# Splitting numbers into a high and a low part: bit masks on VectorE against rounded copies on ScalarE

## The chip, the cores and the metric

The kernel runs on one core of a Trainium2 chip. The metric is the device time of one execution in microseconds (us), the median of several runs. Engines are called as in the profile: PE (TensorE, matmuls), PEld (its weight loads), DVE (VectorE), ACT (ScalarE), POOL (GpSimd), SP (the engine whose queue issues most DMAs).

## The reference

Two blocks follow each other. The first is block-wise linear attention with decay over q, k, v of shape (4 batches, 8 heads, 768 positions, 64 channels). The second is a mixer: a low-rank product along the sequence, added to its input, and a two-layer perceptron over the 512 channels.

```python
for b in range(nb):                                  # attention, blocks of 64
    intra = einsum('bhic,bhjc->bhij', qb, kb) * Dmask
    intra = einsum('bhij,bhjd->bhid', intra, vb)
    inter = einsum('bhid,bhde->bhie', qb * lam_pow, kv_state)
    out[:, :, sl] = intra + inter
    kv_state = lam_block * kv_state + einsum('bhsd,bhse->bhde', kb * rev_pow, vb)
x = out.transpose(0, 2, 1, 3).reshape(4, 768, 512)
u = x + ((x.transpose(0, 2, 1) @ U) @ V).transpose(0, 2, 1)      # rank 32
return u + maximum(u @ w_ch1, 0) @ w_ch2                         # 512 -> 2048 -> 512
```

U, V, w_ch1 and w_ch2 come as 64-bit floats and are brought to 32 bits in the kernel by integer operations on their words.

## The kernel before

**Split products.** The two large products run in the type float32r, which keeps fewer bits of the mantissa than float32. To keep the precision, each operand is split into a high part, which float32r holds exactly, and a low part. Three matmuls replace one: high by high and low by low terms, scaled by E = 2^-12, are gathered in one PSUM bank (`pz`), and a third product of combined parts, `diff` (scaled again by 4096 at the end), in another (`pd`). The high part is made by a bit mask: `tensor_scalar(..., HI, bitwise_and)` with HI = 0xFFFFF000 on VectorE. Splits are made of the weights (`split_steps`: `five` masks, `six` subtracts, `seven` combines), of the transposed input u of the first product (`turn`), and of the hidden values between the two products (`split(i)` near the end).

**Stages.**

1. Attention, from the start to about 113 us. The 24 tiles of 128 positions (4 batches of 6) are 24 steps s; c is the tile's number within its batch. A list written out by hand, `pieces`, fixes the order of instructions on every engine. A step of TensorE runs: transposes of the next tile's q and k (`pqk`, line 363), transposes of an earlier, finished tile (`turn`, line 613) and its neighbour's mix with the low-rank rows (`mix`, line 564), both into one pair of PSUM banks (`pm`), then `intra` (`px`, 452), `state` (`pkv`, 430), `inter` (`px`, 463), `scores` of the next tile (`pss`, 411). From s = 8 to 23 each step has a turn.
2. VectorE in such a step: `masked` (two halves of `sm`, line 420), the mask of the split (633), its subtraction `low` (634), `mixed` (576: x_nat plus the upper halves of `pm`), the new state `kv` (438, or 436 at c = 0), and then, in some steps, an operation of `aside`, a piece of weight preparation. ScalarE: copies of `qt` and `kt` (369), `fade` (404, four small scalings that `kv` needs), weight activations put off to `late`, `x_nat` (469), the scaled high part (620). POOL: `qs` (395), `ks` (384), and `diff` (621), issued by the piece `turned`. At c = 0 there are casts of the low-rank rows (`spread`, 532) as well.
3. `turn` for groups below FG = 4 writes the split of four tiles each into `u_hl` (high and low) and `u_d` (`diff`), laid out as channel block by 512 positions. The last batch's turns (line 595 on) lie between matmuls of the first product and have a bank `put` of their own.
4. First product, to about 420 us: `hidden(ft, pair)` for 16 blocks of hidden channels and three pairs of groups; sums `r` go to DRAM. Weights are prepared beside it.
5. Second product, to the end: `r` comes back, `split(i)` makes `m` (relu, high, low, combined), and `product` adds up 16 blocks.

The PSUM tiles `pkv` and `pqk` share a tag from the second batch on, so the transposes of a step wait until `kv` has read its bank. `tmp` is a ring of three buffers for pieces of splits and for the low-rank rows `p_f` and `p_h`. The weight pieces of the attention stage have their steps in lists:

```python
        (w1_steps(0, True), (3, 4, 5, 6, 8, 9, 10, 11, 13, 14, 15)),
        (w1_steps(1, True, True), (8, 9, 10, 11, 16, 17, 19, 20, 21, 22, 23, NS)),
```

The first four entries of each are loads; then follow `one` (165 and 154; apart in the second list), `two` (183), `three` (191), `four` (196), `five` (214), `six` (222), `seven` (229). ScalarE's part of `one` (172, 173) and of `five` (217) runs one step later, in `late`.

Of the kernel before, what the change touches and what calls it, by code (L numbers as in the profile page):

```python
# [18 lines left out]
def kernel(  # L19
# [43 lines left out]
    TG = N // P  # L63
    HI = 0xFFFFF000
    E = 2.0**-12


    EDGE = 352
# [17 lines left out]
    def on_scalar(what):  # L86
        if late and late[0] is None:
            late.append(what)
        else:
            what()  # L90
# [10 lines left out]
    w2_d = [dram.tile([P, 3, C], FP32, name=f"w2_d{ft}") for ft in range(FT)]  # L101

    def tmp(name):
        return wconv.tile([P, C], FP32, tag="tmp", bufs=3, name=name)

# [94 lines left out]
    def split_steps(tile_of, src, in_parts=False, scale=None, apart=False):  # L202

        st = {}

        def dst():
            if "w" not in st:
                st["w"] = wconv.tile([P, C], FP32, tag="wf", name="wf")
            return st["w"]

        def five():
            st["t"] = t = wconv.tile([P, C], FP32, tag="wt", name="wt")
            st["o"] = o = tile_of()
            nc.vector.tensor_scalar(  # L214
                t.bitcast(U32), st["w"].bitcast(U32), HI, None, ALU.bitwise_and
            )
            on_scalar(lambda: nc.scalar.copy(o[:, 0, :], t))  # L217

        def six():
            w, low = st["w"], st["o"][:, 1, :]  # L220
            st["low"] = low.bitcast(FP32) if scale is None else w
            nc.vector.tensor_tensor(
                out=low if scale is None else w, in0=w, in1=st["t"], op=ALU.subtract
            )
            if scale is not None:
                on_scalar(lambda: nc.scalar.mul(low, w, scale))

        def seven():
            nc.vector.scalar_tensor_tensor(
                st["o"][:, 2, :], st["t"], -E, st["low"], ALU.mult, ALU.add  # L230
            )

        return weight_steps(dst, src, C, in_parts=in_parts, apart=apart) + [five, six, seven]
# [342 lines left out]
        nc.vector.tensor_tensor(out=x, in0=pm, in1=x, op=ALU.add)  # L576

    uhl, ud, turned = {}, {}, {}
    hl_at, d_at = [hl_pool], [d_pool]

    def store(s):
# [2 lines left out]
    def turn(s):  # L584

        g, n = divmod(s, TG)
        if n == 0:
            uhl[g] = hl_at[g >= FG].tile([P, 2, CT, N], F32R, tag="hl", name="u_hl")
            ud[g] = d_at[g >= FG].tile([P, CT, N], F32R, tag="d", name="u_d")
        cols = slice(n * P, (n + 1) * P)  # L590
        hi, low, diff = uhl[g][:, 0, :, cols], uhl[g][:, 1, :, cols], ud[g][:, :, cols]
        if g >= FG:
            pt = bank([P, CT, P], "put", "b1")
            for ct in range(CT):
                nc.tensor.transpose(  # L595
                    out=pt[:, ct, :], in_=xs[s][:, ct * P : (ct + 1) * P], identity=ident
                )
            store(s)
            del xs[s]
            t = tmp("ut").rearrange("p (c n) -> p c n", n=P)  # L600
            nc.vector.tensor_scalar(t.bitcast(U32), pt.bitcast(U32), HI, None, ALU.bitwise_and)

            nc.vector.scalar_tensor_tensor(diff, t, 1.0 + E, pt, ALU.mult, ALU.subtract)
            uf = tmp("uf").rearrange("p (c n) -> p c n", n=P)
            nc.scalar.mul(hi, t, E)
            nc.scalar.copy(uf, pt)
            nc.gpsimd.tensor_tensor(out=low, in0=uf, in1=t, op=ALU.subtract)
            return

        pt = both_halves(s + 1)[:, :, 0 : 2 * P].rearrange("p t (c i) -> p t c i", i=D)  # L610
        for ct in range(CT):
            for n in range(2):
                nc.tensor.transpose(  # L613
                    out=pt[:, n, ct, :], in_=xs[s][half[n], ct * P : (ct + 1) * P],
                    identity=ident[half[n], half[n]],
                )
        del xs[s]

        def rest():
            nc.scalar.mul(hi, t, E)  # L620
            nc.gpsimd.tensor_tensor(
                out=diff, in0=hi.bitcast(FP32), in1=low.bitcast(FP32), op=ALU.subtract
            )

        def parts_of(what):
            return what.rearrange("p c (t i) -> p t c i", t=2)

        t = tmp("ut").rearrange("p (c n) -> p c n", n=P)
        split_t = parts_of(t.bitcast(U32))
        turned[s] = rest  # L630

        def split():
            nc.vector.tensor_scalar(split_t, pt.bitcast(U32), HI, None, ALU.bitwise_and)
            nc.vector.tensor_tensor(
                out=parts_of(low), in0=pt, in1=parts_of(t), op=ALU.subtract
            )

        splits[s] = split
# [4 lines left out]
    for s in range(NS):  # L643
        b, c = divmod(s, NT)
        done = s - NT - 1
        more = s + 1 < NS
        turns = done > 0 and (done - 1) // TG < FG
        mixes = 0 <= done < NS - NT - 1
        rows = c == 0 and b > 0
        step = [("prep", s + 1)] * more  # L650
        step += [("turn", done - 1)] * turns + [("mix", done)] * mixes
        step += [("mix", done + 1)] * (not more)
        step += [("next_of_low", b - 1)] * rows + [("next_of_low", b - 1)] * rows
        step += [("scale", s + 1)] * more
        step += [("fade", s)] * (c > 0)
        step += [("late", s - 1)] * (1 < s < NT - 1 or s > NT)
        step += [("turned", done - 2)] * (done > 1 and c == 1)
        step += [("split", done - 1)] * turns
        step += [("mixed", done)] * mixes + [("mixed", done + 1)] * (not more)
        step += [("next_of_low", b - 1)] * rows  # L660
        both = [("intra", s), ("state", s)]
        step += (both if s > NT else both[::-1]) + [("next_v", s), ("inter", s)]
        step += [("late", s)] * (s < 2 or s in (NT - 1, NT))
        step += [("turned", done - 1)] * (done > 0 and c > 0)
        step += [("scores", s + 1)] * more
        step += [("low", b)] * (more and c == NT - 1)
        step += [("aside", s)] * (0 < s < NT - 2 or s > NT)
        step += [("masked", s + 1)] * more
        step += [("low_rows", b)] * (more and c == NT - 1)
        step += [("aside", s)] * (s in (0, NT - 2, NT - 1, NT))  # L670
        step += [("store", done)] * (done >= 0 and done // TG < FG)
        pieces += step
# [136 lines left out]
    def hidden(ft, pair, before={}):  # L809

        acc = dict(zip(pair, banks(len(pair), next(turns))))
        count = iter(range(12 * len(pair)))

        def others():
            for what, s in before.get(next(count), ()):
                run[what](s)

        w = w1v[ft].rearrange("p n (c f) -> p n c f", f=P)
        for ct in range(CT):
            for n in range(2):  # L820
                for g in pair:
                    others()
                    nc.tensor.matmul(  # L823
                        out=acc[g][0], lhsT=w[:, n, ct, :], rhs=uhl[g][:, n, ct, :],
                        start=(ct == 0 and n == 0), stop=(ct == CT - 1 and n == 1),
                    )
        rs = {g: r_pool.tile([P, N], FP32, tag="r", name="r") for g in pair}
        for g in pair:
            nc.scalar.mul(rs[g], acc[g][0], 4096.0 + 1.0)  # L829
        for ct in range(CT):  # L830
            for g in pair:
                others()
                nc.tensor.matmul(  # L833
                    out=acc[g][1], lhsT=w[:, 2, ct, :], rhs=ud[g][:, ct, :],
                    start=(ct == 0), stop=(ct == CT - 1),
                )
        for g in pair:
            nc.vector.scalar_tensor_tensor(rs[g], acc[g][1], 4096.0, rs[g], ALU.mult, ALU.add)  # L838
            nc.sync.dma_start(out=r_d[ft][g], in_=rs[g])
# [92 lines left out]

    def split(i):
        r = rs.pop(i)
        t = m_pool.tile([P, N], FP32, tag="t", bufs=2, name="mt")
        ms[i] = m = m_pool.tile([P, 3, N], F32R, tag="m", name="m")
        hi, low = m[:, 0].bitcast(FP32), m[:, 1].bitcast(FP32)
        nc.vector.tensor_scalar(t.bitcast(U32), r.bitcast(U32), HI, None, ALU.bitwise_and)  # L938
        nc.scalar.activation(out=m[:, 0], in_=t, func=AF.Relu)  # L939
        nc.vector.scalar_tensor_tensor(m[:, 1], r, 0.0, hi, ALU.max, ALU.subtract)  # L940
        nc.vector.scalar_tensor_tensor(m[:, 2], hi, E, low, ALU.mult, ALU.subtract)  # L941

# [117 lines left out]
```

## Time and profile before

| | |
|---|---|
| Time, median of 3 runs | 650.72 us (649.88 to 652.89) |
| Span of the profiled execution | 648.7 us (its own time is not listed apart) |
| PE busy | 639.9 us, 99% |
| VectorE busy | 489.3 us, 75% |
| ScalarE busy | 279.8 us, 43% |
| POOL busy | 115.5 us, 18% |
| Granted TensorE clock | 1.000 |

The page of the profile gives busy times, a picture in 40 slices, the chain of waits that ended last and the costliest groups of instructions. Behind it stand views of the same trace: windows (busy times by stretch), waits (who waited for whom), and the timeline, whose lines read: start in us, duration in us, engine, line of the kernel, operation, output<-inputs, count, and in brackets the idle time before it and what ended it. A line may gather several instructions in a row on one engine. An instruction's duration may overlap the start of the next.

### The profile page before, as it was taken

To read this page: it belongs to the slowest core of one execution; us is meant where nothing else is said; L and a number is where in the kernel's file an instruction comes from. 1 tells how busy PE (TensorE), PEld (TensorE's weight loads), DVE (VectorE), ACT (ScalarE), POOL (GpSimd) and SP (SyncE) were. 2 spreads that over 40 slices of the span, in tenths; PEclk is the share of its full clock that TensorE was granted. 3 is DMA by queue.
4 is the path that set the end of the run, shared out by engine and by line. 5 is a ranking of instruction groups with operands and counts; after the bars stand their busy time and mean duration, and the time that the engine had idled before them with its cause. 6 is when DMAs were issued, how large, how long until landed. Compare 5 with 4: busy or idle time off the path is not lost.

```text
span 648.7 us, 13400 instructions
## 1 busy us (share of the span) xinstructions
PE 639.9 (99%) x5242; PEld 538.0 (83%) x5242; DVE 489.3 (75%) x862; ACT 279.8 (43%) x530; POOL 115.5 (18%) x98
## 2 busy tenths in 40 slices
PE   9999999999999999999999999999999999999997
PEld 8888989888888888888888888888888888888886
DVE  5579989878999777777797265796677776876864
ACT  4677877554656444444464221332322322322320
POOL 4466868340000000000000000030030300300300
PEclk9999999999999999999999999999999999999999
DMA  9999984354776656566687999855373353453531
GB/s 229 243 239 260 241 206 120 112 194 156 265 266 243 220 209 208 207 211 212 210 292 275 337 321 389 294 181 150 113 213 112 118 199 106 162 162 98 162 99 65
DMA packets 131776, 131.29 MB, mean 202 GB/s; under 512 B 81346, under 2 KB 89794, under 8 KB 131714
## 3 DMA queue, kind: packets, MB, share of 16 engines
q1 hardware_dynamic: 106592, 124.02, 59.7%
q10 hardware_dynamic: 25122, 6.42, 4.4%
q8 instruction: 41, 0.67, 0.4%
q14 instruction: 21, 0.17, 0.1%
HBM read 80.09 MB, written 50.33 MB: 201 GB/s over the span
## 4 chain that ended last, share of the span: by engine, by line
PE 96%; DVE 1%; ACT 1%; DMA 1%; issue 1%; ACTq 0%; DVEq 0%
PE pz L823 27%; PE pd L833 13%; PE pz L956 13%; PE pz L958 13%; PE pd L960 13%; PE pss L411 4%; PE px L452 4%; PE pqk L363 2%; PE px L463 2%; PE pkv L430 1%; PE pp L479 1%; PE pm L564 1%; DMA kraw<-in_k_dram 1%; PE put L595 1%; PE pm L613 0%
## 5 line engine op out<-in xcount | busy, mean ns | idle before, releaser
L823 PE MATMUL pz<-u_hl,w 128*128 128x512 f32 x768 | 184.7, 390 | 0.0
L823 PEld LDWEIGHTS pz<-u_hl,w 128*128 128x128 f32 x768 | 143.5, 188 | 30.4 <-ACT r L829 0.3
L958 PE MATMUL pz<-w_hl,m 128*128 128x512 f32 x384 | 148.3, 389 | 0.0
L956 PE MATMUL pz<-w_hl,m 128*128 128x512 f32 x384 | 148.1, 389 | 0.0
L960 PE MATMUL pd<-w_d,m 128*128 128x512 f32 x384 | 146.7, 389 | 0.0
L939 ACT ACTIVATE m<-mt 128x512 fp32r<-128x512 f32 x96 | 60.6, 632 | 188.3 <-PE pd L960 93.0
L985 POOL TENSOR_TENSOR o<-o,u 128x512 f32<-128x512 f32 x20 | 29.7, 1518 | 432.4 <-DVE o L981 432.4
L838 DVE SCALAR_TENSOR_TENSOR r<-pd,r 128x512 f32<-128x512 f32 x96 | 61.6, 683 | 47.9 <-ACT r L829 41.2
L833 PE MATMUL pd<-u_d,w 128*128 128x512 f32 x384 | 95.9, 390 | 0.0
L940 DVE SCALAR_TENSOR_TENSOR m<-rm,m 128x512 fp32r<-128x512 f32 x96 | 71.2, 744 | 32.4 <-ACT m L939 32.3
L829 ACT ACTIVATE r<-pz 128x512 f32<-128x512 f32 x96 | 52.2, 595 | 87.6 <-PE pz L823 87.6
L960 PEld LDWEIGHTS pd<-w_d,m 128*128 128x128 f32 x384 | 72.1, 188 | 15.3 <-DVE o L981 0.2
L956 PEld LDWEIGHTS pz<-w_hl,m 128*128 128x128 f32 x384 | 72.1, 188 | 15.0
L958 PEld LDWEIGHTS pz<-w_hl,m 128*128 128x128 f32 x384 | 72.1, 188 | 14.8
L833 PEld LDWEIGHTS pd<-u_d,w 128*128 128x128 f32 x384 | 71.8, 188 | 14.8
L938 DVE TENSOR_SCALAR mt<-rm 128x512 uint32<-128x512 uint32 x96 | 46.2, 482 | 39.2 <-DMA rm<-r_d 38.2
L941 DVE SCALAR_TENSOR_TENSOR m<-m 128x512 fp32r<-128x512 f32 x96 | 69.3, 724 | 0.9
L420 DVE TENSOR_TENSOR sm<-pss,mask 128x512 f32<-128x512 f32 x48 | 30.8, 684 | 9.6 <-PE pss L411 9.4
L217 ACT CAST w<-wt 128x512 fp32r<-128x512 f32 x32 | 19.9, 621 | 29.1 <-DVE wt L214 22.4
L452 PE MATMUL px<-vraw,sm 128*64 128x64 f32 x768 | 28.5, 228 | 2.6 <-ACT x_nat L469 1.2
L452 PEld LDWEIGHTS px<-vraw,sm 128*64 128x64 f32 x768 | 25.6, 140 | 5.6 <-ACT x_nat L469 1.5
L411 PE MATMUL pss<-qt,kt 64*128 64x128 f32 x384 | 28.8, 291 | 0.0
(96 smaller groups left out, 668.1 us busy)
## 6 DMA issues: line engine op xcount, KB each, us to landing
r_d<-r SPq DMA_DIRECT2D x96, 256.0 KB, 2.5
rm<-r_d SPq DMA_DIRECT2D x96, 256.0 KB, 2.7
words<-in_moe_w_ch_dram SPq DMA_DIRECT2D x30, 512.0 KB, 4.3
w_d<-w SPq DMA_DIRECT2D x16, 768.0 KB, 3.4
w_hl<-w_d SPq DMA_DIRECT2D x16, 512.0 KB, 6.3
u_d<-x_nat SPq DMA_DIRECT2D x24, 256.0 KB, 4.0
u<-u_d SPq DMA_DIRECT2D x24, 256.0 KB, 4.3
qraw<-in_q_dram SPq DMA_DIRECT2D x23, 256.0 KB, 4.2
```

The lines of the kernel that those rows point to most:

```text
L411: nc.tensor.matmul(out=pss[:, x, a, :], lhsT=kt[half[x], a, :], rhs=qt[half[x], a, :], start=True, stop=True,)
L452: nc.tensor.matmul(out=px[half[t], x, a, :], lhsT=sm[:, x, a, half[t]], rhs=vr[:, 2 * a + x, :], start=(a == 0), stop=(alone and a == HP - 1),
L823: nc.tensor.matmul(out=acc[g][0], lhsT=w[:, n, ct, :], rhs=uhl[g][:, n, ct, :], start=(ct == 0 and n == 0), stop=(ct == CT - 1 and n == 1),)
L829: nc.scalar.mul(rs[g], acc[g][0], 4096.0 + 1.0)
L833: nc.tensor.matmul(out=acc[g][1], lhsT=w[:, 2, ct, :], rhs=ud[g][:, ct, :], start=(ct == 0), stop=(ct == CT - 1),)
L838: nc.vector.scalar_tensor_tensor(rs[g], acc[g][1], 4096.0, rs[g], ALU.mult, ALU.add)
L939: nc.scalar.activation(out=m[:, 0], in_=t, func=AF.Relu)
L940: nc.vector.scalar_tensor_tensor(m[:, 1], r, 0.0, hi, ALU.max, ALU.subtract)
L941: nc.vector.scalar_tensor_tensor(m[:, 2], hi, E, low, ALU.mult, ALU.subtract)
L956: nc.tensor.matmul(out=pz, lhsT=m[:, 0, cols], rhs=hl[:, 0], start=first, stop=False)
L958: nc.tensor.matmul(out=pz, lhsT=m[:, 1, cols], rhs=hl[:, 1], start=False, stop=end)
L960: nc.tensor.matmul(out=pd, lhsT=m[:, 2, cols], rhs=dd, start=first, stop=end)
```

## The change

The mask goes. ScalarE multiplies the value by NEAR = 1 - 2^-13 and writes it into the float32r tile, which rounds it; VectorE subtracts that from the value for the low part.

- Weights: `five` loses its mask and its buffer `wt`; ScalarE's copy becomes a multiply that reads the weight itself; `six` and `seven` read the high part from the output tile.
- Hidden values: ScalarE's relu reads `r` directly, with scale NEAR; the mask and its buffer go.
- Turns of the attention stage: ScalarE writes the high part straight from PSUM, VectorE makes `low` from it and the same PSUM tile. Both now stand in the piece `split`; before, ScalarE's multiplication stood in `turned`, behind `x_nat`. In `pieces`, `mixed` and `split` move ahead of `fade` and `late`, with `mixed` first.
- Turns of the last batch: high on ScalarE from PSUM, `low` on VectorE (before: POOL, from a ScalarE copy), `diff` on POOL (before: VectorE).
- Layout: for groups 0 to 3 the split tiles hold eight runs of 64 positions, each run with its four channel blocks. The moving operand of the first product's matmuls is then eight runs of 64 columns instead of 512 in a row.
- The ring `tmp` has two buffers instead of three.

```diff
     def tmp(name):
-        return wconv.tile([P, C], FP32, tag="tmp", bufs=3, name=name)
+        return wconv.tile([P, C], FP32, tag="tmp", bufs=2, name=name)
...
         def five():
-            st["t"] = t = wconv.tile([P, C], FP32, tag="wt", name="wt")
             st["o"] = o = tile_of()
-            nc.vector.tensor_scalar(
-                t.bitcast(U32), st["w"].bitcast(U32), HI, None, ALU.bitwise_and
-            )
-            on_scalar(lambda: nc.scalar.copy(o[:, 0, :], t))
+            st["t"] = o[:, 0, :].bitcast(FP32)
+            on_scalar(lambda: nc.scalar.mul(o[:, 0, :], st["w"], NEAR))
...
+    def by_halves(what):
+        return what.rearrange("p c n -> p (c n)").rearrange("p (t c i) -> p t c i", c=CT, i=D)
+
+    def columns(what, g, ct):
+        return what[:, ct, :] if g >= FG else by_halves(what)[:, :, ct, :]
...
-            t = tmp("ut").rearrange("p (c n) -> p c n", n=P)
-            nc.vector.tensor_scalar(t.bitcast(U32), pt.bitcast(U32), HI, None, ALU.bitwise_and)
-
-            nc.vector.scalar_tensor_tensor(diff, t, 1.0 + E, pt, ALU.mult, ALU.subtract)
-            uf = tmp("uf").rearrange("p (c n) -> p c n", n=P)
-            nc.scalar.mul(hi, t, E)
-            nc.scalar.copy(uf, pt)
-            nc.gpsimd.tensor_tensor(out=low, in0=uf, in1=t, op=ALU.subtract)
+            nc.scalar.mul(hi, pt, E * NEAR)
+            nc.vector.scalar_tensor_tensor(
+                low, hi.bitcast(FP32), -1.0 / E, pt, ALU.mult, ALU.add
+            )
+            nc.gpsimd.tensor_tensor(
+                out=diff, in0=hi.bitcast(FP32), in1=low.bitcast(FP32), op=ALU.subtract
+            )
             return
...
         def rest():
-            nc.scalar.mul(hi, t, E)
             nc.gpsimd.tensor_tensor(
                 out=diff, in0=hi.bitcast(FP32), in1=low.bitcast(FP32), op=ALU.subtract
             )
...
         def split():
-            nc.vector.tensor_scalar(split_t, pt.bitcast(U32), HI, None, ALU.bitwise_and)
-            nc.vector.tensor_tensor(
-                out=parts_of(low), in0=pt, in1=parts_of(t), op=ALU.subtract
+            nc.scalar.mul(hi, both, E * NEAR)
+            nc.vector.scalar_tensor_tensor(
+                low, hi.bitcast(FP32), -1.0 / E, both, ALU.mult, ALU.add
             )
...
         step += [("scale", s + 1)] * more
+        step += [("mixed", done)] * mixes
+        step += [("split", done - 1)] * turns
         step += [("fade", s)] * (c > 0)
         step += [("late", s - 1)] * (1 < s < NT - 1 or s > NT)
         step += [("turned", done - 2)] * (done > 1 and c == 1)
-        step += [("split", done - 1)] * turns
-        step += [("mixed", done)] * mixes + [("mixed", done + 1)] * (not more)
+        step += [("mixed", done + 1)] * (not more)
...
-                        out=acc[g][0], lhsT=w[:, n, ct, :], rhs=uhl[g][:, n, ct, :],
+                        out=like(acc[g][0], g), lhsT=w[:, n, ct, :],
+                        rhs=columns(uhl[g][:, n], g, ct),
...
-        t = m_pool.tile([P, N], FP32, tag="t", bufs=2, name="mt")
...
-        nc.vector.tensor_scalar(t.bitcast(U32), r.bitcast(U32), HI, None, ALU.bitwise_and)
-        nc.scalar.activation(out=m[:, 0], in_=t, func=AF.Relu)
+        nc.scalar.activation(out=m[:, 0], in_=r, func=AF.Relu, scale=NEAR)
```

More of the change, by code (lines that the diff above doesn't have):

```diff
@@ L65 @@
     E = 2.0**-12
+    NEAR = 1.0 - 2.0**-13
     EDGE = 352
@@ L578, with like @@
     uhl, ud, turned = {}, {}, {}
+    def by_halves(what):
+        return what.rearrange("p c n -> p (c n)").rearrange("p (t c i) -> p t c i", c=CT, i=D)
+    def columns(what, g, ct):
+        return what[:, ct, :] if g >= FG else by_halves(what)[:, :, ct, :]
+    def like(out, g):
+        return out if g >= FG else out.rearrange("p (t i) -> p t i", i=D)
     hl_at, d_at = [hl_pool], [d_pool]
@@ L589, in turn @@
             ud[g] = d_at[g >= FG].tile([P, CT, N], F32R, tag="d", name="u_d")
-        cols = slice(n * P, (n + 1) * P)
-        hi, low, diff = uhl[g][:, 0, :, cols], uhl[g][:, 1, :, cols], ud[g][:, :, cols]
         if g >= FG:
+            cols = slice(n * P, (n + 1) * P)
+            hi, low, diff = uhl[g][:, 0, :, cols], uhl[g][:, 1, :, cols], ud[g][:, :, cols]
             pt = bank([P, CT, P], "put", "b1")
@@ L599, in turn @@
             del xs[s]
-            t = tmp("ut").rearrange("p (c n) -> p c n", n=P)
-            nc.vector.tensor_scalar(t.bitcast(U32), pt.bitcast(U32), HI, None, ALU.bitwise_and)
-            nc.vector.scalar_tensor_tensor(diff, t, 1.0 + E, pt, ALU.mult, ALU.subtract)
-            uf = tmp("uf").rearrange("p (c n) -> p c n", n=P)
-            nc.scalar.mul(hi, t, E)
-            nc.scalar.copy(uf, pt)
-            nc.gpsimd.tensor_tensor(out=low, in0=uf, in1=t, op=ALU.subtract)
-            return
-        pt = both_halves(s + 1)[:, :, 0 : 2 * P].rearrange("p t (c i) -> p t c i", i=D)
+            nc.scalar.mul(hi, pt, E * NEAR)
[5 more added lines that the diff above has]
+            )
+            return
+        hi, low, diff = (
+            by_halves(what)[:, 2 * n : 2 * n + 2].rearrange("p t c i -> p t (c i)")
+            for what in (uhl[g][:, 0], uhl[g][:, 1], ud[g])
+        )
+        both = both_halves(s + 1)[:, :, 0 : 2 * P]
+        pt = both.rearrange("p t (c i) -> p t c i", i=D)
         for ct in range(CT):
@@ L623, in rest @@
             )
[L625 to L629, printed above, removed]
         turned[s] = rest
         def split():
-            nc.vector.tensor_scalar(split_t, pt.bitcast(U32), HI, None, ALU.bitwise_and)
-            nc.vector.tensor_tensor(
-                out=parts_of(low), in0=pt, in1=parts_of(t), op=ALU.subtract
+            nc.scalar.mul(hi, both, E * NEAR)
+            nc.vector.scalar_tensor_tensor(
+                low, hi.bitcast(FP32), -1.0 / E, both, ALU.mult, ALU.add
             )
@@ L833, in hidden @@
                 nc.tensor.matmul(
-                    out=acc[g][1], lhsT=w[:, 2, ct, :], rhs=ud[g][:, ct, :],
+                    out=like(acc[g][1], g), lhsT=w[:, 2, ct, :], rhs=columns(ud[g], g, ct),
                     start=(ct == 0), stop=(ct == CT - 1),
```

## The prediction

> **What bounds the kernel now.** The page comes first: the span, the engines, the chain that ended last.
>
> ```profile
> span 648.7 us, 13400 instructions
> PE 639.9 (99%) x5242; PEld 538.0 (83%) x5242; DVE 489.3 (75%) x862; ACT 279.8 (43%) x530; POOL 115.5 (18%) x98
> PE 96%; DVE 1%; ACT 1%; DMA 1%; issue 1%; ACTq 0%; DVEq 0%
> ```
>
> TensorE is the chain. In its list of pieces, matmuls of 512 columns follow each other without a gap from 142.19 us to 644.17 us, at 5.44 us per 24 (227 ns each). No split is late there, so a cheaper one gains nothing there. What can move is the attention stage, up to 113 us. The windows by stage show who is nearly as busy as TensorE:
>
> ```profile
> 50.00:75.00 25.00, 24.53 (x689) 22.50 (x686) 23.39 (x40) 19.89 (x48) 18.72 (x17) 1.00 1.01 251
> 175.00:200.00 25.00, 25.00 (x112) 20.70 (x111) 24.73 (x47) 15.68 (x28) 0.00 (x0) 1.00 0.74 260
> ```
>
> (Columns: stretch, its length, busy us of PE, PEld, DVE, ACT, POOL; then clock, DMA.) VectorE is busy for 23.39 of 25 us, ScalarE for 19.89, POOL for 18.72. All run in the order written out in `pieces`. So I read the timeline of one step, s = 10, which begins with `pqk` at T = 52.30 in the chain; the next begins at 56.60. The period is 4.30.
>
> ```profile
> 52.35 1.29 DVE L420 TENSOR_TENSOR sm<-pss,mask 128x512 f32<-128x512 f32 x2 [0.16 <-PE pss L411]
> 53.37 0.59 ACT L369 COPY kt<-pqk 128x512 f32<-128x512 f32 x1
> 53.56 0.68 DVE L633 TENSOR_SCALAR ut<-pm 128x512 uint32<-128x512 uint32 x1
> 53.85 1.07 ACT L404 ACTIVATE faded<-kv,powq 128x64 f32<-128x64 f32 x4
> 54.27 0.69 DVE L634 TENSOR_TENSOR u_hl<-pm,ut 128x512 fp32r<-128x512 f32 x1
> 54.88 0.68 DVE L576 TENSOR_TENSOR x_nat<-pm,x_nat 128x512 f32<-128x512 f32 x1
> 55.48 0.41 DVE L438 TENSOR_TENSOR kv<-pkv,faded 128x256 f32<-128x256 f32 x1
> 55.53 1.07 POOL L384 TENSOR_TENSOR ks<-kraw,small 128x512 f32<-128x512 f32 x1
> 55.81 1.35 DVE L191 SCALAR_TENSOR_TENSOR sc<-words,sc 128x512 uint32<-128x512 uint32 x1
> 57.85 0.36 PE L452 MATMUL px<-vraw,sm 128*64 128x64 f32 x5 [0.22 <-ACT qt L369]
> ```
>
> VectorE never waits after the mask, and its step ends with a weight operation of `aside`. L191 usually takes 0.69; here it took 1.35, because POOL's `ks` ran until 56.60: it ended 0.56 after that. L222 at 74.43 (1.39, `ks` until 75.27) and L229 at 125.10 (1.50, POOL until 126.06) do the same: a VectorE operation with two SBUF inputs that comes second waits for POOL's. The mask then ran until about 57.75, and TensorE, which needs its first half, lost 0.22 (the release shown, `qt`, isn't what it reads). Such stalls, 0.22 here and 0.23 at 76.52, are all that a lighter VectorE could win back in these steps.
>
> The step after a batch's end (s = 12) has another tight place:
>
> ```profile
> 63.57 0.42 DVE L524 TENSOR_SCALAR p_h<-p_f 32x512 uint32<-32x512 uint32 x1
> 64.07 1.66 ACT L532 CAST vp<-p_h 32x256 fp32r<-32x256 f32 x4
> 65.95 0.41 DVE L436 COPY kv<-pkv 128x256 f32<-128x256 f32 x1
> 66.41 0.33 PEld L363 LDWEIGHTS pqk<-ident,qraw 64*128 64x128 f32 x8 [0.26 <-DVE kv L436]
> ```
>
> `pkv` and the next `pqk` share banks, so TensorE waits for VectorE's `kv`.
>
> Last, what two engines do that both read one PSUM tile (`put`):
>
> ```profile
> 132.94 0.69 DVE L603 SCALAR_TENSOR_TENSOR u_d<-ut,put 128x512 fp32r<-128x512 f32 x1
> 133.74 0.59 ACT L606 COPY uf<-put 128x512 f32<-128x512 f32 x1 [0.16 <-DVE u_d L603]
> ```
>
> ScalarE reads only `put` and writes a buffer of its own, yet starts only when VectorE's read has ended (133.63), here and at 128.63 and 140.55. Reads of one PSUM tile by two engines are put in program order.
>
> **The change part by part.** *Second product.* 96 masks x 0.482 = 46.3 us of VectorE go; L956 and L958 show no idle TensorE that these release: 0.
>
> *Weights.* 32 masks x 0.433 = 13.9 us of VectorE go; ScalarE's 32 copies (0.621) become multiplies (nearest row L226, 0.637): +0.5 us beside TensorE. VectorE's `six` now waits for ScalarE; queued behind it are the r sums of L838. The two PSUM sets cover that: 0; if that cover is gone, up to 0.6 on each of 30 tiles, 18 us, which only the 24.73-of-25 stretch above makes thinkable.
>
> *Last batch's turns.* 8 masks (0.69) and 8 ScalarE copies (0.59) go; `low` changes from POOL to VectorE and is ready earlier; `diff` goes to POOL (1.29) but is needed only by L833. TensorE's one wait for POOL's L607 (0.3) goes: -0.3.
>
> *The layout of groups 0 to 3.* 4 groups x 16 x 12 = 768 matmuls now read eight runs of 64 columns. No row shows this. Lower end 0, as the columns stay 512. Upper end from L613: eight transposes of 64 columns take 0.25 us, against 0.227 for one matmul: 23 ns x 768 = 18 us. I take 0, by the 512-column row, whose column count and contiguous PSUM output it keeps. The Trainium skill (SBUF - State Buffer, "Door 1: The DMA port swizzle") says that reads run at full speed inside lines of 16 bytes, which by itself gives 0 for runs of 256 bytes; no run here shows it.
>
> *The ring `tmp`*, 3 to 2: only `p_f` and `p_h` of each batch still use it, one buffer each: 0.
>
> *The turns in the attention stage*, steps 8 to 23. 16 masks (0.68) go. But ScalarE's high part moves ahead of `fade`, and three things queue behind it. Step 10, from T: the mask's two halves start at 0.05 and 0.65, `mixed` at 1.26, ending at 1.94. ScalarE is free after `kt` at 1.55, but by the `put` row its read waits for `mixed`: 2.00 to 2.63 (0.59 from PSUM in L606, 0.63 with an fp32r output in L620; I take 0.63). `low` 2.70 to 3.39. `fade` starts 0.48 behind the high part, at 2.48, and ends at 3.55. `kv` 3.62, before 3.18. Up to here nothing is late: the next mask is due at 4.35.
>
> Then the weight operation. Before, POOL's `diff` waited for the late high part and ran at 53.07, beside PSUM work. Now it is free once `low` is done, 3.45 (or after `ks`, 3.79), for 1.28, and the weight operation becomes free at 3.95, behind it. It waits until 4.73 and takes 0.56 more: 5.29. One round of VectorE is then 5.25 instead of 4.30. Steps with such an operation, a state and a turn, by the lists `at`: 8, 9, 10; 14, 15, 16; 19, 20, 21. The mask has 1.04 - 0.73 = 0.31 of slack to the next `px` and starts 0.05 late: three rounds in a row lose 3 x 0.95 - 0.26 = 2.6; the middle group ends with a single short operation (L165), 2.4. Sum 7.6, less the 0.45 already lost there: **+7.1**. Upper end, with `diff` behind `ks` in each group's first step: 3 x 0.34 = 1.0 more.
>
> Steps 12 and 18: in ScalarE's queue the high part stands behind the four L532 casts: 65.60 to 66.23, `low` until 66.98, `kv` at 66.92 to 67.33. `pqk` starts at 67.38 instead of 66.42: 0.96. In step 18 `kv` ended just in time; the same sum gives 0.93. **+1.9**.
>
> Step 17: ScalarE's two exponent activations (L172, L173) come behind the high part, so `x_nat` ends at T + 4.5, and `pp` needs it at 4.2: **+0.3**.
>
> Sum: 7.1 + 1.9 + 0.3, less 0.3 of the last turn: +9.0. Nothing behind takes it back, since TensorE has no gap to close up. The profiled execution has no time of its own in the list; its span of 648.7 lies 2.0 below the median of the runs, 650.72, and I leave that margin as it is: 648.7 + 9.0 + 2.0 = **659.7**.
>
> One rule speaks against this change from another side. Row: ScalarE copies 512 PSUM columns in 0.587 (L606), VectorE masks them in 0.691 (L601). The Trainium skill (ScalarE: Activation LUTs, "Rules for kernel authors") would leave multiply and relu to VectorE; by that each moved split would be dearer, by the row it is 0.1 cheaper. The row decides; what costs is the place in the queue.
>
> **The rivals.** *The operations meet, but VectorE comes first* (0.12). If `diff` starts after 3.95, POOL waits instead. The round is then 3.95 + 0.63 - 0.05 = 4.53, and a group loses 3 x 0.23 - 0.26 = 0.4; `x_nat` of step 9 is late behind L172 and L173 (0.4). With steps 12, 17 and 18 and the last turn: 1.2 + 0.4 - 0.45 + 2.2 - 0.3 = +3.1, **653.8**. For it: with `ks` ahead the margin in a first step is only 0.16 (3.79 against 3.95). Against: in later rounds `low` is late with the mask, and `diff` starts 0.5 ahead of the weight operation.
>
> *No order between the two readers* (0.14). The high part runs at 1.55, `kv` at 3.1, and the weight operation ends by 4.4 even behind `ks` (until 3.79, then 0.56): no group loses more than before. Steps 12, 17 and 18 and the last turn remain: 2.2 - 0.3 = +1.9, **652.6**. For it: `put` shows the order for two reads that touch the same columns; in `pm` the high part and `mixed` read different columns of one tile.
>
> *The other side: the lighter VectorE wins* (0.13). This is so if the high part finds ScalarE free in steps 12 and 18 too, `kv` ends by 3.6 and `diff` leaves the weight operation alone. Then the stalls of 0.22, 0.23 and 0.26 and the 0.3 of the last turn go: -1.0, **649.7**. For it: VectorE loses 0.68 per step. Against: it gets a wait of 0.7 for ScalarE in return (1.94 to 2.70). All stalls of steps 12 to 19, over what the pieces of a step add up to, are about 3 us, so more than 0.5% is nearly out of reach.
>
> *The reads in runs cost* (0.07): up to 18 us on top of the forecast, **678**; each nanosecond per matmul is 0.8 us. Only the bound from L613 speaks for it.
>
> **How the numbers follow.** The forecast has 0.54. Its own range is 656 to 662: the 1.0 of `ks` above, and below it a group or two that VectorE wins. The next two rivals reach down to 652.6, and 651 is about as far below that as the lowest run lies below the median (0.8); the last two lie outside, so 651 to 664 leaves out 0.2. About 0.5%, 3.25 us, is what a measurement here tells from no change (the three times lie 0.46% apart). Slower: 0.54, half of 0.12, and 0.07: 0.67. Same: 0.06 + 0.14 + 0.10 = 0.30. Faster: the 0.03 that is left of the lighter VectorE.
>
> **What would show it.** Right: `u_hl` on ScalarE starting 0.06 after `mixed` ends; `kv` waiting for `faded`; L183, L191, L222, L229 at over 1 us in the nine steps, with TensorE waiting before `px`; `pqk` waiting about 1 us for `kv` after steps 12 and 18; matmuls still at 227 ns; nothing lost after 143 us. Wrong: high parts ahead of `mixed`, steps of 4.30 with a weight operation, or 512-column matmuls off 5.44 us per 24.

## The result, and the profile after

The changed kernel takes 658.7 us (median of 4 runs, 657.85 to 659.18); the kernel before, beside it, 650.3 us (median of 4: the three runs above and one more). The ratio is 1.0117, with a 95% interval of 1.0095 to 1.0138: 8.4 us slower. The forecast was 659.7 us, 9.0 above the kernel before.

The page of the changed kernel (span, engines, chain):

```profile
span 656.0 us, 13415 instructions
PE 640.0 (98%) x5242; PEld 537.9 (82%) x5242; DVE 438.6 (67%) x710; ACT 276.4 (42%) x522; POOL 115.7 (18%) x98
PE 94%; ACT 3%; issue 1%; DVE 1%; DMA 1%; DVEq 0%; ACTq 0%
```

TensorE does the same work (640.0 us against 639.9), VectorE has 50.7 us less (438.6 against 489.3), and the span is 7.4 us longer (656.04 against 648.67). The chain now passes through ScalarE for 3% instead of 1%. The windows by stage show where:

```profile
50.00:75.00 25.00, 22.50 (x622) 20.57 (x622) 18.32 (x31) 17.91 (x42) 16.11 (x14) 1.00 0.87 220
175.00:200.00 25.00, 25.00 (x112) 20.71 (x111) 24.13 (x44) 15.98 (x27) 0.00 (x0) 1.00 0.75 268
```

In the attention stage every engine, TensorE too, is now less busy (PE 22.50 of 25 us, 24.53 before; VectorE 18.32, 23.39 before): they wait for each other. In the first product nothing changed for TensorE.

Step 8 in the timeline of the changed kernel, with `pqk` beginning at T = 42.93 in the chain (in the changed file `mixed` is L574, the high part L639, `low` L640, `kv` L436, `diff` L632, `ks` L382):

```profile
44.18 0.68 DVE L574 TENSOR_TENSOR x_nat<-pm,x_nat 128x512 f32<-128x512 f32 x1
44.90 0.60 ACT L639 ACTIVATE u_hl<-pm 128x512 fp32r<-128x512 f32 x1 [0.31 <-DVE x_nat L574]
45.53 0.69 DVE L640 SCALAR_TENSOR_TENSOR u_hl<-u_hl,pm 128x512 fp32r<-128x512 f32 x1 [0.66 <-ACT u_hl L639]
45.66 1.06 POOL L382 TENSOR_TENSOR ks<-kraw,small 128x512 f32<-128x512 f32 x1 [0.20 <-POOL qs L393]
46.48 0.42 DVE L436 TENSOR_TENSOR kv<-pkv,faded 128x256 f32<-128x256 f32 x1 [0.26 <-ACT faded L402]
46.68 1.28 POOL L632 TENSOR_TENSOR u_d<-u_hl 128x512 fp32r<-128x512 f32 x1
46.82 1.42 DVE L166 TENSOR_SCALAR sc<-words 128x512 uint32<-128x512 uint32 x1
49.27 1.24 PE L450 MATMUL px<-vraw,sm 128*64 128x64 f32 x32 [1.01 <-ACT kt L367]
```

ScalarE's read of `pm` starts 0.04 us after `mixed` has ended (44.86); `low` waits 0.66 us for it; `kv` waits for `faded`; POOL's `diff` starts 0.14 us before the weight operation L166, which then takes 1.42 us (0.43 before); and TensorE waits 1.01 us at the next `px`, whose first mask began only at 48.49. (As before, the profile names `kt`; what was late is the mask.)

Step 12, behind a batch's end:

```profile
65.53 0.69 DVE L574 TENSOR_TENSOR x_nat<-pm,x_nat 128x512 f32<-128x512 f32 x1
65.59 1.66 ACT L530 CAST vp<-p_h 32x256 fp32r<-32x256 f32 x4
67.28 0.60 ACT L639 ACTIVATE u_hl<-pm 128x512 fp32r<-128x512 f32 x1
67.91 0.69 DVE L640 SCALAR_TENSOR_TENSOR u_hl<-u_hl,pm 128x512 fp32r<-128x512 f32 x1 [1.68 <-ACT u_hl L639]
68.51 0.42 DVE L434 COPY kv<-pkv 128x256 f32<-128x256 f32 x1
68.98 0.40 PE L361 MATMUL pqk<-ident,qraw 64*128 64x64 f32 x6 [1.12 <-DVE kv L434]
```

The high part stands behind the four casts, and the next `pqk` waits 1.12 us for `kv`.

Step by step, from the start of one step's scores (`pss`) to the next, read from the timelines; the last four columns are runs explained below:

| step | before | after | attention turns alone | diff off POOL | weight operation moved | casts moved, two on POOL |
|---|---|---|---|---|---|---|
| 9, 10, 11 | 4.30, 4.30, 4.22 | 5.46, 5.06, 4.58 | 5.37, 5.05, 4.58 | 4.46, 5.09, 3.83 | 4.64, 4.39, 3.92 | 5.46, 5.05, 4.59 |
| 13 | 4.58 | 5.64 | 5.69 | 5.63 | 5.57 | 4.62 |
| 14, 15, 16 | 4.32, 4.78, 5.08 | 4.30, 4.58, 5.05 | 5.07, 5.40, 5.05 | 4.30, 4.58, 4.44 | 4.29, 4.30, 4.62 | 4.30, 5.34, 5.05 |
| 17, 18 | 4.22, 5.53 | 4.32, 6.26 | 4.32, 6.20 | 4.06, 6.26 | 3.84, 5.75 | 4.32, 6.26 |
| 19 | 4.53 | 5.65 | 5.70 | 5.64 | 5.41 | 4.62 |
| 20, 21, 22 | 4.30, 4.30, 4.30 | 5.34, 5.39, 5.05 | 5.35, 5.39, 5.05 | 4.39, 4.44, 4.43 | 4.30, 4.30, 4.80 | 4.92, 5.17, 5.05 |
| 8 to 23 | 72.39 | 80.30 | 82.49 | 75.18 | 73.81 | 78.36 |

(A weight operation that is late in step s lengthens step s + 1. The last row ends where the first product's first `pz` begins.) The attention stage loses 7.91 us.

### The profile page after: what moved, and what is told of

Read it like the earlier page. It is cut to its first block, busy times and chain, and to the rows that moved or that the text cites. A ratio compares the mean times of both kernels' runs of the same rounds, so it can differ in the third digit from the quotient of the medians.

```text
span 656.0 us, 13415 instructions
## 1 busy us (share of the span) xinstructions
PE 640.0 (98%) x5242; PEld 537.9 (82%) x5242; DVE 438.6 (67%) x710; ACT 276.4 (42%) x522; POOL 115.7 (18%) x98
## 4 chain that ended last, share of the span: by engine, by line
PE 94%; ACT 3%; issue 1%; DVE 1%; DMA 1%; DVEq 0%; ACTq 0%
PE pz L830 26%; PE pz L964 13%; PE pz L962 13%; PE pd L966 13%; PE pd L841 13%; PE px L450 4%; PE pss L409 3%; PE pqk L361 2%; PE px L461 2%; PE pkv L428 1%; ACT qt L367 1%; PE pp L477 1%; DMA qraw<-in_q_dram 1%; PE put L603 0%; ACT vp L530 0%
## 5 line engine op out<-in xcount | busy, mean ns | idle before, releaser
L945 ACT ACTIVATE m<-rm 128x512 fp32r<-128x512 f32 x96 | 60.6, 632 | 182.6 <-PE pd L966 124.4
L947 DVE SCALAR_TENSOR_TENSOR m<-m 128x512 fp32r<-128x512 f32 x96 | 74.7, 779 | 3.0
L215 ACT ACTIVATE w<-wf 128x512 fp32r<-128x512 f32 x32 | 20.3, 633 | 35.9 <-DVE wf L197 28.1
L173 ACT ACTIVATE sc<-sc,ends 128x512 f32<-128x512 uint32 x30 | 21.6, 720 | 23.9 <-DVE sc L166 23.9
```

Source lines behind the costliest of these rows:

```text
L945: nc.scalar.activation(out=m[:, 0], in_=r, func=AF.Relu, scale=NEAR)
```

## Experiments: which part, and by what

Ratios are to the kernel before, in runs on the same chip.

**Everything but the attention turns** (`e_rest`): the kernel before, with these edits of the change alone.

```diff
 five:  - mask to wt; scalar.copy(o, wt)            + scalar.mul(o, w, NEAR)
 turn, g >= FG: - mask, diff on DVE, low on POOL    + high on ACT, low on DVE, diff on POOL
 split(i):      - mask; relu(t)                     + relu(r, scale=NEAR)
```

> The kernel before with the changed splits of the weights, the hidden values and the last batch's turns; the turns of the attention stage, their layout and the order of pieces as before. Theory (the loss lies in the attention steps, in what queues behind ScalarE's high part): 650.3 plus the 0.5 us that the profile after shows between 122 and 152 us, 650 to 652. Rival (the splits outside the attention stage, or ScalarE's work in general, carry the loss): 655 or more.

651.24 us, ratio 0.9978 (0.9961 to 0.9995). The loss isn't here. The interval lies just below 1, but the trace shows no shorter stretch (steps 8 to 23 take 72.98 us, 72.39 before), so a gain isn't claimed. Its stretch from the first `pz` to the end of the first product's fourth unit (the sixth piece of `pd` in the chain) is 29.65 us, as in the changed kernel (29.67), against 29.11 before.

**The attention turns alone** (`e_turns`): the other half, with the new order of pieces and the new layout.

```diff
 split(s): - mask, subtract on DVE      + scalar.mul(hi, both, E * NEAR); low on DVE
 pieces:   - fade, late, split, mixed   + mixed, split, fade, late
 matmuls:  - rhs=uhl[g][:, n, ct, :]    + rhs=columns(uhl[g][:, n], g, ct)
```

> The kernel before with the attention stage's turns alone changed: ScalarE's high part from PSUM, the new order of pieces and the new layout; weights, hidden values and the last batch's turns keep their masks. Theory (the loss is made in these steps): 7 to 10 us over before, a ratio of 1.011 to 1.015, with the masks of the weights in steps 13 and 22 as two more VectorE operations that can meet POOL's diff. Rival (the parts hurt only together): under 1.008.

661.2 us, ratio 1.0150 (1.0124 to 1.0177). The half that holds the attention turns loses more than the whole: steps 14 to 16 take 15.52 us here (13.93 in the changed kernel), because the masks of the weights are still on VectorE: the mask of step 13 (74.43) took 1.36 us behind `diff`, and the subtraction after it (79.54) came second as well and took 1.65.

**Weights and hidden values alone** (`e_weights`): as `e_rest`, with the last batch's turns unchanged.

> The kernel before with only the weights' and the hidden values' masks gone; all turns as before. Theory: TensorE has no gap that these could close, so within 0.2% of before, and the 0.5 us that the run with all outside the attention stage loses between its first pz and 30 us later is absent. Rival (VectorE's 60 us less is worth something by itself): 2 us or more below before.

650.93 us, ratio 0.9993 (0.9975 to 1.0011). The masks that go add up to 60 us, and VectorE's busy time falls by 40.0 us (449.3 against 489.3); that is worth nothing that can be measured. The stretch from the first `pz` is 29.07 us. So the half microsecond of `e_rest` belongs to the last batch's turns.

**`diff` off POOL** (`e_nopool`): the changed kernel, where the operand of the third product is a copy of the low part, so one subtraction is left out.

```diff
-            nc.gpsimd.tensor_tensor(out=diff, in0=hi, in1=low, op=ALU.subtract)
+            nc.scalar.copy(diff, low)
```

> The changed kernel, with diff of the attention turns written as a plain copy of the low part by ScalarE instead of POOL's subtraction (the value of that operand is left wrong; instruction counts on PE and VectorE stay). Theory (weight operations of VectorE stand behind POOL's diff at the shared port): weight operations take 0.69 again instead of 1.3, a round of VectorE 4.53 instead of 5.25, steps 9 to 11 and 20 to 22 lose 1.0 together instead of 5.2; 654 to 656. Rival (VectorE's wait for ScalarE alone makes the round too long): 658 to 659.

654.53 us, ratio 1.0037 (1.0024 to 1.0050). Two weight operations of it, from the timeline:

```profile
101.62 0.68 DVE L184 SCALAR_TENSOR_TENSOR m<-words,m 128x512 f32<-128x512 uint32 x1
106.05 0.69 DVE L192 SCALAR_TENSOR_TENSOR sc<-words,sc 128x512 uint32<-128x512 uint32 x1
```

The first of them in the changed kernel, with the `diff` that it met (two `diff` in one line):

```profile
103.05 2.96 POOL L632 TENSOR_TENSOR u_d<-u_hl 128x512 fp32r<-128x512 f32 x2
103.25 1.63 DVE L184 SCALAR_TENSOR_TENSOR m<-words,m 128x512 f32<-128x512 uint32 x1
```

Steps 9 to 11 and 20 to 22 lose 0.56 + 0.36 = 0.92 us against before, instead of 2.28 + 2.88 = 5.16. (The 0.56 stem from step 10, 0.79 longer, where 0.39 is a wait of TensorE that the profile calls "issue".) VectorE's wait for ScalarE is still there (0.66 each time); the round it leaves, 4.39 to 4.44 us, is nearly short enough. So it is POOL's place at the port that costs, not the wait alone.

**The weight operation moved into that wait** (`e_gap`):

```diff
         step += [("mixed", done)] * mixes
-        step += [("split", done - 1)] * turns
+        step += [("high", done - 1)] * turns      # ScalarE's part
+        step += [("aside", s)] * (turns > 0)      # was ahead of masked
+        step += [("split", done - 1)] * turns     # VectorE's part
```

> The changed kernel, with the weight operation of a step (the piece aside) moved on VectorE from behind kv to between mixed and low, where VectorE waits 0.66 us for ScalarE. Theory: it then meets POOL's qs (until T + 2.53) and not diff, ends by T + 3.1, low by 3.8, kv by 4.2, and the step keeps 4.3: steps 9 to 11 and 20 to 22 win back about 4.5 of 5.2 us, 653 to 655. Rival (the operations collide wherever they stand, as POOL is busy 3.6 of 4.3 us): 657 to 660.

653.55 us, ratio 1.0027 (1.0006 to 1.0049). In step 10 of it:

```profile
56.54 1.24 DVE L192 SCALAR_TENSOR_TENSOR sc<-words,sc 128x512 uint32<-128x512 uint32 x1
57.70 0.68 DVE L642 SCALAR_TENSOR_TENSOR u_hl<-u_hl,pm 128x512 fp32r<-128x512 f32 x1
58.65 1.27 POOL L632 TENSOR_TENSOR u_d<-u_hl 128x512 fp32r<-128x512 f32 x1
```

L192 still waits, now for POOL's `qs` (until 57.23), but VectorE had to wait there anyway. Steps 9 to 11 and 20 to 22 lose 0.13 + 0.50 = 0.63 us: 4.53 of 5.16 are won back with all the work in place.

**The casts behind the high part** (`e_spread`):

```diff
-        step += [next_of_low] * 2 ... mixed, split     # casts, POOL's rows, then the high part
+        step += [next_of_low] ... mixed, split, [next_of_low]   # POOL's rows, high part, casts
```

> The changed kernel, with the four L530 casts of a batch's low-rank rows moved in ScalarE's queue from before the high part to behind it (and POOL's subtraction for them ahead). Theory: the high part of steps 12 and 18 starts right after mixed instead of 1.0 to 1.1 us later, kv ends that much earlier, pqk waits at most 0.2: -1.6 to -2.2 us, 656.5 to 657.1. Rival (pqk is late there for another reason, such as pp or the rows on VectorE): no change, 658.7.

659.37 us, ratio 1.0101 (1.0085 to 1.0117): a miss; steps 13 and 19 take 5.44 and 5.43, 0.2 less. The reason stands in its timeline:

```profile
67.61 0.69 DVE L574 TENSOR_TENSOR x_nat<-pm,x_nat 128x512 f32<-128x512 f32 x1
68.34 0.60 ACT L639 ACTIVATE u_hl<-pm 128x512 fp32r<-128x512 f32 x1 [0.66 <-DVE x_nat L574]
69.57 0.42 DVE L434 COPY kv<-pkv 128x256 f32<-128x256 f32 x1
70.50 0.83 ACT L541 CAST vp<-vp 32x256 fp32r<-32x256 f32 x2
70.81 0.95 PE L562 MATMUL pm<-vp 64*128 64x256 f32 x4
72.00 1.15 PE L450 MATMUL px<-vraw,sm 128*64 128x64 f32 x32 [0.23 <-ACT x_nat L467]
```

As expected the high part starts 0.04 us after `mixed` has ended (68.30), and `kv` ends 1.0 us earlier in its step; `pqk`, at 70.05, hardly waits. But now the last casts, L541, run until 71.33, the next mix that needs them takes 0.95 us instead of 0.48, and `x_nat` is late for `px`. What stood ahead of the high part is late in its turn.

**Two of the casts on POOL** (`e_spread_pool`): the same, with

```diff
-                nc.scalar.copy(place(2 * x + 1, 1), place(2 * x, 1).bitcast(FP32))
+                nc.gpsimd.tensor_copy(out=place(2 * x + 1, 1), in_=place(2 * x, 1).bitcast(FP32))
```

> As the run with the four casts behind the high part, and the two casts that follow them (L541) are copies on POOL, ahead of its qs. Theory (in steps 12 and 18 ScalarE's queue is full: whatever stands in front, what stands behind is late, so moving the casts back only moved the wait from pqk to the mix and x_nat): with 0.83 us off ScalarE, steps 13 and 19 fall from 5.4 us to 4.6 to 4.9, 1.2 us or more below the changed kernel, 657 to 657.8. Rival (the rows themselves are late, from VectorE's p_h on): 5.4 again.

657.36 us, ratio 1.0079 (1.0051 to 1.0108), and steps 13 and 19 take 4.62 and 4.62 us (before: 4.58 and 4.53). With 0.83 us taken off ScalarE the loss is gone: ScalarE's queue was full in these steps, and the change had moved its high part from the end of that queue into the middle. Elsewhere the order at the port came out otherwise: step 15 takes 5.34 instead of 4.58, as the weight operation of step 14 met the start of `ks` (1.45 us; 0.69 in the changed kernel), and steps 20 and 21 take 0.42 and 0.22 less.

**Moves that should pay for themselves.** The turn of tile 17 behind mix 18 in the first unit, without the attention turns (`e_rest_order`) and with them and the moved weight operation (`e_gap_order`); and all moves together (`e_all`):

```diff
-        (0, 18, "turn", c0 - 1), (0, 22, "mix", c0),
+        (0, 22, "mix", c0), (0, 23, "turn", c0 - 1),
```

> The kernel before with all splits changed outside the attention stage, and the turn of tile 17 moved behind mix 18 in the first unit of the first product, so that VectorE's sum L570 no longer stands behind low, which waits for ScalarE. Theory: put no longer waits for x_nat, the stretch from the first pz to the end of unit 3 takes 28.9 us as before instead of 29.5; ratio to before 0.995 to 0.999. Rival (put waits there for the casts of the rows whatever the order): 29.5, as without the move.

> The changed kernel with both moves: the weight operation between mixed and low, and the turn of tile 17 behind mix 18. Theory: the gains add up, 0.5 us below the run with the first move alone, a ratio to before of 1.000 to 1.003; what is left are steps 12, 13, 18 and 19, where ScalarE is full. Rival: no better than the first move alone.

> The changed kernel with all moves together: the weight operation between mixed and low, the casts behind the high part with the last two on POOL, the turn of tile 17 behind mix 18. Theory: no place with over 0.3 us of loss is left in steps 8 to 23, which take 71.5 to 72.5 us; ratio to before 0.996 to 1.000. Rival (the moves meet at POOL, which gets 1.6 us more in steps 12 and 18): 1.001 or more.

`e_rest_order`: 650.28 us, ratio 0.9983 (0.9965 to 1.0001). The stretch from the first `pz` takes 29.27 us instead of 29.65; `put` no longer waits for `x_nat` (0.8 us on PEld in `e_rest`), but 0.5 us of PEld's waiting for the casts (`pu`) has come in its place, so 28.9 was not reached. `e_gap_order`: 651.79 us, ratio 1.0014 (0.9995 to 1.0034), the stretch 29.29 instead of 29.64, within the expectation's range. Its gain over `e_gap` is smaller than the two intervals can tell. `e_all`: 651.65 us, ratio 0.9984 (0.9963 to 1.0005). Steps 8 to 23 take 73.70 us, over the expected 72.5: in steps 10, 12, 14 and 15 its TensorE waited 1.6 us in all (0.20, 0.66, 0.25 and 0.47) for nothing that the profile shows ("issue"). The change can thus be had at no cost that can be measured; that any of these beats the kernel before isn't shown, since all three intervals hold 1.

## Why the prediction was right, and where it was not

*By the clock of one step.* For step 10 the forecast gave `mixed` at T + 1.26, the high part 2.00, `low` 2.70, `kv` 3.62, `diff` 3.79 behind `ks`, the weight operation 3.95. Step 8 of the changed kernel, the first of the nine steps, has 1.25, 1.97, 2.60, 3.55, 3.75 and 3.89. Both disputed points hold: the read of `pm` by ScalarE waits for VectorE's `mixed` (14 times, 13.0 us in the waits), though the columns differ; and POOL comes first. The margin of the second was the 0.14 us that the forecast had called thin (0.16).

*By the terms of the sum.*

| term | forecast | measured |
|---|---|---|
| first group of weight operations (steps 9 to 11) | +2.4 | +2.28 |
| second group (14 to 16) | +2.2 | -0.25 |
| third group (20 to 22) | +2.6 | +2.88 |
| casts ahead of the high part (12 and 18, seen in 13 and 19) | +1.9 | 1.06 + 1.12 = +2.18 |
| exponents before `x_nat` (17, seen in 17 and 18) | +0.3 | +0.83 |
| last batch's turns | -0.3 | 29.67 - 29.11 = +0.56 |
| elsewhere | 0 | -0.8 before step 8, -0.3 behind |
| sum, spans | +9.0 | +7.4 |

That the total comes so near (658.7 us against 659.7) is in part luck. The second group came out 2.45 us below its term and the steps outside the terms 1.1 below; the last batch came out 0.86 above, the exponents 0.53, the casts and the third group 0.28 each. By medians the loss is 8.4 us and not 7.4, mainly because the profiled execution was the fastest of the four (657.85). One bound of the forecast doesn't follow from its own words: 651 lies 1.6 us below the rival's 652.6, twice the 0.8 that it names.

*The second group* failed twice. `six` (L220) stood in the queue while `ks` still held the port, so VectorE went next, ahead of `diff`; this is the rival in which VectorE comes first, in one of the nine steps:

```profile
76.61 1.05 POOL L382 TENSOR_TENSOR ks<-kraw,small 128x512 f32<-128x512 f32 x1
77.57 0.69 DVE L220 TENSOR_TENSOR w<-wf,w 128x512 fp32r<-128x512 f32 x1
77.62 1.78 POOL L632 TENSOR_TENSOR u_d<-u_hl 128x512 fp32r<-128x512 f32 x1
```

So the group loses 1.03 us over three free steps (4.30 each, without a wait), where the forecast had 2.4. And the kernel before had lost 0.48 us in step 15 and 0.78 in step 16, of which 0.47 are an unexplained "issue" wait of TensorE; the forecast had counted only the stall of 0.23 at 76.52. Where `diff` came first, in `e_turns`, the group takes 15.52 us, 2.62 over three free steps, though with the mask of step 13 as a fourth operation.

*The exponents* were mis-sized: `x_nat` ended at 92.37, T + 4.9 in step 17 and not T + 4.5, as VectorE's round entered the step late from step 16's weight operation; each step was summed as if it began on time. This is read from the trace alone; no run takes the exponents out.

*The last batch* had the wrong sign. POOL's wait did go, as said. But the sum L570, which makes the input of the next `put`, stands behind `low` on VectorE, and `low` behind ScalarE's casts and r sums:

```profile
130.53 0.60 ACT L608 ACTIVATE u_hl<-put 128x512 fp32r<-128x512 f32 x1
131.17 0.69 DVE L609 SCALAR_TENSOR_TENSOR u_hl<-u_hl,put 128x512 fp32r<-128x512 f32 x1 [2.28 <-ACT u_hl L608]
131.77 0.69 DVE L570 TENSOR_TENSOR x_nat<-pu,x_nat 128x512 f32<-128x512 f32 x1
132.51 0.66 PE L603 MATMUL put<-ident,x_nat 128*128 128x128 f32 x4 [0.38 <-DVE x_nat L570]
```

The forecast asked who needs `low` and `diff`, not who is queued behind the new wait. (`put` waits 0.38 here; with the turn moved, in `e_rest_order`, that wait is gone and the stretch 0.38 shorter.)

*What cost nothing, as said.* The weights and hidden values (`e_weights`: 0.9993), and the reads in eight runs: 24 matmuls still take 3.63 + 1.81 = 5.44 us in the chain.

*The port.* L166 (0.43 before) took 1.42 beside `diff`, L184 1.31 and 1.63. The Trainium skill (SBUF — State Buffer, "SBUF: two separate sides") says that the ports VectorE shares with GpSimd are locked by whoever starts first, for its whole instruction, against VectorE operations with two SBUF inputs or in a two-port mode. The trace agrees: every late one ended a fixed time after POOL's, 0.55 us where it takes 0.68 by itself, and 0.28 for L166. That L166, which has one SBUF input, runs in such a mode isn't shown.

## What to carry to other kernels

Work that is taken off a busy engine is worth only what the last wait of its stage was worth; here that was under 1 us, and 50.7 us less on VectorE bought nothing. When an operation moves to another engine, walk both queues: list what now stands behind it, and who waits for that, before counting what was saved. A step that has 0.3 us of slack is decided by which of two engines reaches a shared port first, so where an idle gap opens in a queue, put there the operation that would collide elsewhere.

## What the runs showed of the hardware

- A single-input VectorE operation (L166, 0.43 alone) is held by a POOL operation as well: 1.42 us. The other way round, POOL's `diff`, 1.28 by itself, took 1.78 behind VectorE's L220.
- ScalarE writes 512 float32r values from PSUM in 0.597 us (L639), from SBUF it took 0.632 (L620 before).
- Profiles of kernels whose first seven steps issue nearly the same work differ by 2.8 us in when step 8 is reached (41.77 to 44.58 us), and up to there and behind it TensorE shows waits called "issue" of 0.2 to 1.7 us, at places that change from one profile to the next. What causes them stays open. A difference of 1 us between two single profiles is no finding; the step table carries its verdicts because the same steps move by the same amount in several runs.
